# Filler products in TensorE's waits, selections transposed by DMA and new load prices in a planned attention and FFN kernel

## The chip, the cores and the metric

The kernel runs on one core of a Trainium2 chip. The metric is the device time of one execution in microseconds; before the change its median is 272.86 us over 8 runs (271.62 to 273.15).

## The reference

Inputs are q, k and v (batch 4, 8 heads, 768 positions, head size 64) and two weight matrices. Attention selects, for every query, 6 of the 24 key chunks of 32 positions, by an upper bound of the scores, and then attends causally to these chunks alone. Its output, 3,072 tokens of 512 values, goes through an FFN of width 2,048 with a squared ReLU.

```python
k_min, k_max = min and max of k over each chunk of 32
ub = sum_d max(q * k_min, q * k_max)             # bound per query and chunk
ub = where(causal, ub, -1e9)
top_chunks = argsort(ub)[..., -6:]
scores = q @ k.T / 8, where the key's chunk is selected and the key is not later
attn = softmax(scores) @ v
h = maximum(x @ w_in, 0)
out = (h * h) @ w_out
```

## The kernel before

**Tiles.** A sequence is cut into 6 tiles of 128 positions. The first tile of each sequence has fewer than 6 earlier chunks, so it needs no selection: `first_attention` handles it alone for all four sequences, and the FFN of these four tiles (`x_first`) runs first. The remaining five tiles are handled in 16 head pairs (4 sequences of 4 pairs). For each pair `stage_a` prepares and `stage_b` attends.

**Stage A** has this chain: keys and queries transposed (kT, qT), chunk minima and maxima (kr, DVE), positive and negative parts of the queries (qp, qm), the bounds by TensorE (ub), the mask (ubm), the best eight by DVE (m), the comparison that writes the 0/1 selection (selb, L628), its transpose (sT, `turn_selection`, L574 and L632: three TensorE transposes into a PSUM buffer of tag "ps"), and four copies (`copy_selection`, L578) into rows 64 to 87 of the query operand qsc. There a product with −32768 in the key operand kqc switches off the chunks that are not selected. For sequences 0 and 1 keys and queries are transposed by TensorE; for 2 and 3 (`BY_DMA = 2`) by DMA transposes that SP issues (`turn_by_dma`, L328), from staging buffers of tag "nt", of which there are six, or for the first keys from the tile `k0` (`load_turned`, L353).

**Stage B** does, for each head, five score blocks of 512 columns (ps, L679), exponentials by ACT (e, L701), causal masking by DVE or GpSimd, values (av, L690), and the division (x, L521). **The FFN** transposes x (xt, or by DMA for sequences 1 and 2), then `up` (ph, L763; ReLU on ACT or DVE; the square h on DVE) and `down` (py, L793; copy ob; store by SP). For the four first tiles `up` runs in two halves of 256 tokens.

**Order.** Nothing is ordered by hand. Class `Plan` holds every operation with its possible engines and costs, its due time, its inputs and its buffers. `order()` simulates the five engines, the buffer slots of each tag and a single DMA queue, and takes the operation that can start first, among near ties the one due first. The program is written in the order of planned starts, and each engine executes its own part strictly in that order. The planner has these prices: a TensorE operation that starts before `WARM` = 23.5 us costs double (L118); a load takes 0.98 ns a packet (L124), in the order of the string `loads` (i and o are blocks of w_in and w_out, q, k, v are head pairs of sequence 0, F the first tiles of sequences 2 and 3). At most eight GpSimd loads are in flight (L98). `lead` says how long before a pair's stage B its stage A is due; 20 units are one pair. `f_due` is the due time of the first attention of sequences 2 and 3, and `half` is the number of w_in blocks of 128 columns that the first FFN handles in halves. At the very start `warm_up` issues eight products of the all-ones tile `warm`.

The steps below touch L118 to L125 (planner), L145 (`write`), L185 (`P`), L328 to L369 (DMA transposes), L386 to L395 (weight loads), L450 to L458 (warm-up), L545 and L632 (selection).

Of the kernel before, what the change touches and what calls it, by code (L numbers as in the profile page):

```python
# [32 lines left out]
class Op:  # L33
    def __init__(self, where, due, fn, needs, tiles, packets, turns):
        self.where, self.due, self.fn, self.turns = where, due, fn, turns
        self.needs, self.tiles, self.packets = needs, tiles, packets
        self.engine = None
        self.start = self.end = None


class Plan:
# [7 lines left out]
    HAND_OVER = {"PE": 0.22, "ACT": 0.10, "DVE": 0.10, "POOL": 0.12, "SP": 0.1}  # L49
    BUSY = 0.09  # L50
    WAIT = 0.06
    WARM = 23.5
    NEVER = 1e9

    def __init__(self, slots):
        self.slots = slots
        self.ops = []
        self.loads = []

# [10 lines left out]
    def order(self):  # L70
        free = {e: 0.7 for e in ("PE", "ACT", "DVE", "POOL", "SP")}
        slots = {tag: [0.0] * n for tag, n in self.slots.items()}
        waiting = {}
        count = {}
        for op in self.ops:
            for t in op.tiles:
                t.left = len(t.users)
            count[op] = len(op.needs)
            for n in op.needs:
                waiting.setdefault(n, []).append(op)  # L80
        ready = [op for op in self.ops if not count[op]]
        landed, queue, done = [], 0.0, []
        while ready:
            found = []
            for op in ready:
                if op.packets and not op.turns and op is not self.loads[len(landed)]:
                    continue
                at = 0.0
                new = {}
                for t in op.tiles:  # L90
                    if not t.held:
                        new[t.tag] = new.get(t.tag, 0) + 1
                for tag, n in new.items():
                    at = max(at, sorted(slots[tag])[n - 1]
                             if n <= len(slots[tag]) else self.NEVER)
                if at == self.NEVER:
                    continue
                if op.packets and not op.turns and len(landed) >= 8:  # L98
                    at = max(at, landed[-8])
                for engine, cost in op.where.items():  # L100
                    st = max(at, free[engine])
                    for n in op.needs:
                        same = n.engine == engine and not n.packets
                        lag = (0.0 if engine == "PE" else self.BUSY) if same                             else self.HAND_OVER[n.engine]
                        st = max(st, n.end + lag)
                    for t in op.tiles:
                        if t.psum:
                            for e, end in t.last.items():
                                if e != engine and "PE" not in (e, engine):
                                    st = max(st, end + self.HAND_OVER[e])  # L110
                    found.append((st, op, engine, cost))
            assert found, "nothing can start"
            first = min(found, key=lambda f: f[0])
            st, op, engine, cost = min(
                (f for f in found if f[2] == first[2] and f[0] <= first[0] + self.WAIT),
                key=lambda f: (f[1].due, f[0]))
            ready.remove(op)
            if engine == "PE" and st < self.WARM:  # L118
                cost *= 2
            op.engine, op.start, op.end = engine, st, st + cost  # L120
            free[engine] = op.end
            if op.packets:
                queue = max(queue, op.end + (0.7 if op.turns else 1.3))
                queue += op.packets * 0.00098  # L124
                op.end = queue + (0.85 if op.turns else 0.35)  # L125
                if not op.turns:
                    landed.append(op.end)
            for t in op.tiles:
                if not t.held:
                    t.held = True  # L130
                    slots[t.tag].remove(min(slots[t.tag]))
                t.last[engine] = max(t.last.get(engine, 0.0), op.end)
                t.left -= 1
                if not t.left:
                    slots[t.tag].append(
                        max(u.end + self.HAND_OVER[u.engine] for u in t.users))
            for n in waiting.get(op, ()):
                count[n] -= 1
                if not count[n]:
                    ready.append(n)  # L140
            done.append(op)
        assert len(done) == len(self.ops), "operations left"
        return sorted(done, key=lambda op: op.start)

    def write(self):  # L145
        for op in self.order():
            for t in op.tiles:
                if t.tile is None:
                    t.tile = t.make()
            op.fn(op.engine)  # L150


@with_exitstack
def kernel(
# [9 lines left out]
    nc = tc.nc  # L164
# [17 lines left out]
    QC = 128 * NS  # L182
    VW = 80
    NSET = 4
    P = dict(lead=[26, 30, 30, 22, 30, 30, 30, 30, 30, 28, 34, 30, 30, 26, 28, 30],  # L185
             f_due=-123.64, up_due=-21.43, up_rate=3.78, half=10,
             due=[6, 16, 14, 6], rate=[2.42, 2.39, 2.73, 2.66],
             va=5.42, vm=1.3, ra=0.29, h2=1.53,
             loads="i0 q0 k0 F v0 i2 i1 k1 q1 v1 k2 "
                   "v2 o0 q3 i3 q2 k3 o1 v3 o3 o2")  # L190

    nc.scalar.preload_act_table_set("natural_log_exp_and_others")

# [13 lines left out]
    plan = Plan({"tp": 1, "ps": 3, "av": 2, "ff": 2, "e": 6, "h2": NFI + 6, "ht": 3,  # L207
                 "ob": 3, "kq": 6, "nt": 6,
                 "vn": B - 1, "x": 2, "xT": 2,
                 "kr": 2, "qp": 2, "qm": 2, "ubm": 2, "m8": 2, "rc": 2})  # L210
    POOLS = {"tp": pst, "ps": pss, "av": psav, "ff": psf, "e": epool, "h2": hpool,
             "ht": hpool, "ob": opool, "vn": ld, "nt": ldt, "kq": tpool}

# [111 lines left out]
                turned[nm, b] = buffer("kq", [128, NT if nm == "k" else NS, NP, 128],  # L325
                                       name=nm + "t")

    def turn_by_dma(dst, src, due, needs, tiles):  # L328
        return plan.op({"SP": 1.2}, due, lambda _: nc.sync.dma_start_transpose(
            out=dst(), in_=src()), needs, tiles, packets=1070, turns=True)  # L330

    def load_by_sp(nm, due):

# [19 lines left out]
    def load_turned(nm, b, j, due):  # L353
        dst = turned[nm, b]
        if j == 0:
            src, needs = None, loaded[nm, b, "first"]
        else:
            src = buffer("nt", [128, H, D])
            load((nm, b, j), lambda _: nc.gpsimd.dma_start(
                out=src.tile,  # L360
                in_=SRC[nm][b, :, 128 * j:128 * (j + 1)].rearrange("h p d -> p h d")),
                due, 1024, [src])
            needs = loaded[nm, b, j]
        i = j if nm == "k" else j - 1
        op = turn_by_dma(
            lambda: dst[:, i],
            lambda: (src.tile if src else firsts[nm][:, b]).rearrange(
                "p h d -> p (h d)"), due, needs, [src, dst])
        loaded.setdefault((nm, b), []).append(op)  # L369
# [14 lines left out]
    def load_w_in(f0, f1, due):  # L384
        cols = slice(128 * f0, 128 * f1)
        load(("in", f0 // 4), lambda _: nc.gpsimd.dma_start(  # L386
            out=w_in_sb[:, :, cols],
            in_=moe_w_in[:, cols].rearrange("(ki p) f -> p ki f", p=128)),
            due, 2450, cost=0.76)

    def load_w_out(f0, f1, due):
        load(("out", f0 // 4), lambda _: nc.gpsimd.dma_start(
            out=w_out_sb[:, f0:f1],
            in_=moe_w_out[128 * f0:128 * f1].rearrange("(fi p) d -> p fi d", p=128)),
            due, 2450, cost=0.76)  # L395

    def key_tile(nm, b, hp, j):
        t = firsts[nm][:, b] if j == 0 else nat[nm, b][:, j - 1]
# [32 lines left out]
    for b in range(1, B):  # L431
        ones(b, 20 * NP * b - 70)
        for i, nm in enumerate("kq"):
            for j in range(1, NT) if b < BY_DMA else ():
                load_tile(nm, b, j, 20 * NP * b - 70 + 5 * i + j)
            for j in range(0 if nm == "k" else 1, NT) if b >= BY_DMA else ():
                load_turned(nm, b, j, 20 * NP * b - 70 + 5 * i + j)
        for j in range(1, NT):
            load_tile("v", b, j, 20 * NP * b - 60 + j)
# [7 lines left out]
    t_first = {}  # L447
    x_done = {}

    def warm_up(n):  # L450

        wt = psav.tile([128, 4, 128], F32, tag="av", name="wt")
        for _ in range(n):
            nc.tensor.matmul(wt, lhsT=warm,
                             rhs=warm.unsqueeze(1).to_broadcast([128, 4, 128]),
                             start=True, stop=True)

    made["warm"] = plan.op({"PE": 1.7}, -999, lambda _: warm_up(8), [made["vector"]])  # L458

    def first_transposes(nm, b, tag, due):  # L460
        pt = buffer(tag, [128, NP, 128], name="T0")
# [68 lines left out]
    def stage_a(p):  # L530
# [11 lines left out]
        ub = buffer("ps", [128, NS, 2, NC], F32, name="ub")  # L542
        ubm = buffer("ubm", [128, NS, 2, NC], F32)
        m8 = buffer("m8", [128, NS, 2, 8], F32)
        sT = buffer("ps", [128, NT // 2, 128], name="sT")  # L545

        def part(t, rows=slice(0, 128)):
            return t[rows, :, hp] if b >= BY_DMA else t[rows]
# [62 lines left out]
        else:  # L611
# [17 lines left out]
            selbs[:, s, 0:NS, :, 0:NC], ubm.tile,  # L629
            m8[:, :, :, TOPK - 1:TOPK].to_broadcast([128, NS, 2, NC]),  # L630
            op=ALU.is_lt), m + prepared.get((p - NSET, "sT"), []), [ubm, m8])
        t = op({"PE": 0.17}, t0 + 21, turn_selection, [sel, made["ident"]], [sT])  # L632
        prepared[p, "sT"] = [t]
        cs = [[op({"DVE": 0.33, "ACT": 0.385}, t0 + 23 + 2 * hh,
                  lambda e, hh=hh, i=i: copy_selection(e, hh, i),
# [248 lines left out]
```

## Time and profile before

| | |
|---|---|
| median of 8 runs | 272.86 us |
| profiled execution | 272.9 us, of it span 271.2 us |
| mean granted TensorE clock | 0.98 |
| busy PE / DVE / ACT / POOL | 254.6 / 201.8 / 179.6 / 102.7 us |
| chain that ended last | PE 48%, DVE 39%, DMA 8% |
| loads by GpSimd's queue | 13.37 MB in 77,088 packets |

The span runs from the first to the last instruction of one profiled execution. Busy time of PE is matmul time; matmuls are pipelined, so two that overlap are counted once, and a busy PE need not be one at its peak rate. PEld is the loading of the stationary operand, beside it. The granted clock is the share of full speed that the throttle gave TensorE. Rows of groups give line, engine, operation, output and input with shapes, the count, total busy time and the mean of one in ns. Rows of the timeline begin with start and duration in us and end with the idle time before them and what released it.

### The profile page before, as it was taken

The numbers are of one execution on the slowest core, as the hardware profiler recorded it, in microseconds if no ns is written. First come the engines' busy times: TensorE is split into PE (matmuls) and PEld (weight loads), VectorE is DVE, ScalarE is ACT, GpSimd is POOL, SyncE is SP. The second block draws the span as 40 slices with busy tenths as digits, with TensorE's granted clock in tenths as the row PEclk, the third lists the DMA queues.
The fourth block names the chain that finished last, engine by engine and source line by source line (L and its number), as shares of the span: only waits on it lengthen the run. The fifth ranks groups of instructions, "written<-read, shape, count | busy, mean of one in ns | idle before, by whom it ended". The sixth has DMA issues, their size and how long they took to land.

```text
span 271.2 us, 6595 instructions
## 1 busy us (share of the span) xinstructions
PE 254.6 (94%) x2424; PEld 165.0 (61%) x2424; DVE 201.8 (74%) x712; ACT 179.6 (66%) x359; POOL 102.7 (38%) x176
## 2 busy tenths in 40 slices
PE   7478799999999999999899999999999999999994
PEld 2255685666678766555577665567866556665441
DVE  4468699988999999999999999665899524345000
ACT  4356699968888888566578886556888634467111
POOL 8885688898459935812122221001111100000000
PEclk9859999999999999999999999999999999999999
DMA  9999999999999998991520001183000020110111
GB/s 120 180 164 176 137 142 181 195 156 193 172 153 117 152 141 88 164 145 41 116 60 2 2 0 41 41 119 98 2 0 2 1 80 39 41 40 0 41 77 77
DMA packets 100301, 25.07 MB, mean 92 GB/s; under 512 B 92932, under 2 KB 97196, under 8 KB 100268
## 3 DMA queue, kind: packets, MB, share of 16 engines
q0 software_dynamic: 77088, 13.37, 67.6%
q1 hardware_dynamic: 23180, 11.27, 19.9%
q8 instruction: 19, 0.31, 0.5%
q14 instruction: 14, 0.11, 0.1%
HBM read 27.26 MB, written 6.29 MB: 124 GB/s over the span
## 4 chain that ended last, share of the span: by engine, by line
PE 48%; DVE 39%; DMA 8%; POOL 2%; issue 2%; ACT 1%; DVEq 0%; POOLq 0%; ACTq 0%
PE py L793 21%; PE ph L763 16%; DMA w_in_sb<-in_moe_w_in_dram 8%; DVE kr L598 8%; DVE h L781 6%; PE ps L679 5%; DVE qsc L225 4%; DVE kqc L225 4%; PE av L690 3%; DVE m L572 3%; DVE ht L772 3%; DVE x L521 3%; DVE qp L614 2%; DVE qm L614 1%; DVE selb L628 1%
## 5 line engine op out<-in xcount | busy, mean ns | idle before, releaser
L701 ACT ACTIVATE e<-ps 128x512 bf16<-128x512 f32 x160 | 92.8, 598 | 23.9 <-PE ps L679 20.5
L763 PE MATMUL ph<-xT,w_in_sb 128*128 128x256 bf16 (+2 forms) x616 | 101.6, 300 | 2.5 <-DMA w_in_sb<-in_moe_w_in_dram 1.9
L793 PE MATMUL py<-w_out_sb,h 128*128 128x512 bf16 x384 | 95.0, 379 | 0.0
L763 PEld LDWEIGHTS <-w_in_sb 128*128 128x128 bf16 x616 | 57.9, 98 | 25.2 <-DMA w_in_sb<-in_moe_w_in_dram 2.4
L659 POOL TENSOR_SCALAR_AFFINE_SELECT e<-e 128x128 bf16<-128x128 bf16 (+1 forms) x85 | 29.9, 354 | 101.0 <-ACT e L701 99.2
L770 ACT ACTIVATE ht<-ph 128x256 bf16<-128x256 f32 (+2 forms) x113 | 49.7, 443 | 20.3 <-PE ph L763 17.2
L781 DVE TENSOR_TENSOR h<-ht 128x256 bf16<-128x256 bf16 (+2 forms) x154 | 48.1, 326 | 19.5 <-ACT ht L770 12.7
L679 PE MATMUL ps<-qsc,kqc 88*128 88x128 bf16 (+1 forms) x320 | 59.6, 272 | 1.0 <-ACT qsc L223 1.0
L793 PEld LDWEIGHTS <-h 128*128 128x128 bf16 x384 | 35.5, 97 | 30.6
L690 PEld LDWEIGHTS <-e 128*128 128x128 bf16 x640 | 39.1, 97 | 17.7 <-DVE e L656 0.9
L690 PE MATMUL av<-vn,e 128*128 128x65 bf16 x480 | 39.9, 193 | 0.3 <-DVE e L656 0.3
L223 ACT COPY ob<-py 128x512 f32<-128x512 f32 x23 | 13.5, 585 | 24.2 <-PE py L793 24.2
L679 PEld LDWEIGHTS <-kqc 88*128 88x128 bf16 x320 | 24.0, 98 | 6.7 <-issue 1.1
L772 DVE TENSOR_SCALAR ht<-ph 128x256 bf16<-128x256 f32 (+1 forms) x41 | 18.8, 464 | 1.4 <-PE ph L763 1.1
L521 DVE TENSOR_TENSOR x<-av,rc 128x320 bf16<-128x320 f32 (+1 forms) x40 | 18.9, 471 | 0.6
L656 DVE TENSOR_TENSOR e<-e,tri 128x128 bf16<-128x128 bf16 (+1 forms) x43 | 10.0, 235 | 8.5 <-ACT e L701 8.1
L223 ACT COPY qsc<-sT 24x256 bf16<-24x256 bf16 (+1 forms) x31 | 12.8, 414 | 4.5 <-DVE qsc L225 2.9
L572 DVE MAX8 m<-ubm 128x8 f32<-128x24 f32 x160 | 15.6, 166 | 0.1
L690 PE MATMUL av<-v,e 128*128 128x65 bf16 x160 | 15.3, 193 | 0.0
L598 DVE TENSOR_REDUCE kr<-kT 128x24 bf16<-128x768 bf16 x16 | 14.9, 947 | 0.1
L598 DVE TENSOR_REDUCE kr<-kt 128x24 bf16<-128x768 bf16 x16 | 14.7, 939 | 0.1
L372 POOL DMA_DIRECT2D vn<-in_v_dram x15 | 13.2, 903 | 0.1
(83 smaller groups left out, 243.7 us busy)
## 6 DMA issues: line engine op xcount, KB each, us to landing
out_dram<-ob SPq DMA_DIRECT2D x24, 256.0 KB, 2.0
w_in_sb<-in_moe_w_in_dram POOLq DMA_DIRECT2D x4, 512.0 KB, 9.6
w_out_sb<-in_moe_w_out_dram POOLq DMA_DIRECT2D x4, 512.0 KB, 8.0
vn<-in_v_dram POOLq DMA_DIRECT2D x15, 128.0 KB, 6.8
nt<-in_k_dram POOLq DMA_DIRECT2D x10, 128.0 KB, 7.3
nt<-in_q_dram POOLq DMA_DIRECT2D x10, 128.0 KB, 4.9
qn<-in_q_dram POOLq DMA_DIRECT2D x8, 80.0 KB, 8.5
kn<-in_k_dram POOLq DMA_DIRECT2D x8, 80.0 KB, 7.9
```

Source lines behind the costliest of these rows:

```text
L223: nc.scalar.copy(dst, src)
L521: return plan.op({"DVE": 0.06 + 0.00108 * D * n}, due, lambda _: nc.vector.tensor_mul(x(), av[:, :, 0:D], rc[:, 0:n].unsqueeze(2).to_broad ...
L598: nc.vector.tensor_reduce(kr[:, mm].rearrange("d (t c) -> d t c", c=128 // CH) if b >= BY_DMA else kr[:, mm], part(kT).rearrange("d t (c j ...
L659: nc.gpsimd.affine_select(out=e, in_=e, compare_op=ALU.is_ge, fill=0.0, base=0, channel_multiplier=-1, pattern=[[0, n], [1, 128]])
L679: nc.tensor.matmul(ps[:, 128 * c:128 * (c + nt)], lhsT=kqs[:, s, hh, 128 * j:128 * (j + 1)], rhs=qss[:, s, hh, 128 * (t0 - 1):128 * (t0 - ...
L690: nc.tensor.matmul(av[:, t - 1], lhsT=e[:, 128 * c:128 * (c + 1)], rhs=value_tile(b, h, j), start=(i == 0 and c == 0), stop=(i == len(BANK ...
L701: nc.scalar.activation(e.tile, ps.tile, ACT.Exp, scale=scale), [sc], [ps, e])
L763: nc.tensor.matmul(ph.tile, lhsT=w_in_sb[:, ki, 128 * f:128 * (f + 1)], rhs=xT[:, c0 // 128:c1 // 128, ki], start=(ki == 0), stop=(ki == N ...
L770: nc.scalar.activation(ht.tile, ph.tile, ACT.Relu)
L772: nc.vector.tensor_scalar_max(ht.tile, ph.tile, 0.0)
L781: {"DVE": 0.067 + w / 1920}, at[0] + P["h2"], lambda _: nc.vector.tensor_mul(h2[f][:, c0:c1], ht.tile, ht.tile), [op], [ht, h2[f]])))
L793: nc.tensor.matmul(py.tile, lhsT=h2[f][:, 128 * t:128 * (t + 1)], rhs=w_out_sb[:, f, :], start=(f == 0), stop=(f == NFI - 1))
```

## The change

The planner counts double cost for TensorE only before 8 us. For a TensorE operation that starts before 26 us and takes a new PSUM buffer, it notes how many products of 0.216 us fit between the moment when engine and buffer are free and the operation's start, less 0.3 us. Before such an operation is written, `keep_warm` writes that many products of the all-ones tile into its buffer: matmuls for f32 buffers, four times as many transposes for bf16 buffers. The first warm-up has nine products instead of eight. A load takes 0.83 ns a packet; a w_in block counts 4,150 packets, a w_out block 3,070, a DMA transpose 1,270. The order of loads and the due times are different. The first keys of sequences 2 and 3 are transposed by DMA after those of tile 1 have been loaded, not as soon as they are there. The selections of sequences 2 and 3 are transposed by a DMA that SP issues, into a buffer of tag "nt" in SBUF.

```diff
-    WARM = 23.5
+    WARM = 8.0
+    FILL = 26.0
...
-            if engine == "PE" and st < self.WARM:
-                cost *= 2
+            if engine == "PE":
+                op.fill = 0
+                if st < self.FILL and op.tiles:
+                    room = max([free[engine]] + [
+                        sorted(slots[t.tag])[0] for t in op.tiles
+                        if t.psum and not t.held])
+                    op.fill = max(0, int((st - room - 0.3) / 0.216))
+                if st < self.WARM:
+                    cost *= 2
...
-                queue += op.packets * 0.00098
+                queue += op.packets * 0.00083
...
+            if op.fill:
+                self.keep_warm([t for t in op.tiles if t.psum][0].tile, op.fill)
             op.fn(op.engine)
...
-    P = dict(lead=[26, 30, 30, 22, 30, 30, 30, 30, 30, 28, 34, 30, 30, 26, 28, 30],
-             f_due=-123.64, up_due=-21.43, up_rate=3.78, half=10,
-             due=[6, 16, 14, 6], rate=[2.42, 2.39, 2.73, 2.66],
-             va=5.42, vm=1.3, ra=0.29, h2=1.53,
-             loads="i0 q0 k0 F v0 i2 i1 k1 q1 v1 k2 "
-                   "v2 o0 q3 i3 q2 k3 o1 v3 o3 o2")
+    P = dict(lead=[18, 24, 28, 20, 32, 28, 28, 26, 24, 30, 36, 32, 36, 30, 32, 32],
+             f_due=-222.1, up_due=-24.77, up_rate=4.07, half=11, due=[10, 24, 24, 20],
+             rate=[2.42, 2.62, 2.73, 2.11], va=9.67, vm=0.89, ra=-0.27, h2=0.69,
+             loads="i0 q0 k0 F i2 v0 k1 i1 q1 v2 i3 "
+                   "v1 k2 o0 q2 q3 k3 o1 v3 o2 o3")
...
-    def turn_by_dma(dst, src, due, needs, tiles):
+    def turn_by_dma(dst, src, due, needs, tiles, packets=1270):
...
-            src, needs = None, loaded[nm, b, "first"]
+            src, needs = None, loaded[nm, b, "first"] + loaded[nm, b, 1]
...
+    def keep_warm(dst, n):
+        size = 1
+        for dim in dst.shape[1:]:
+            size *= dim
...
+        if dst.dtype == F32:
+            size = min(size, 512) // 128 * 128 or size
+            for _ in range(n * 512 // size):
+                nc.tensor.matmul(
+                    dst[:, 0:size].rearrange("p (a b) -> p a b", b=min(size, 128)),
+                    lhsT=warm, rhs=warm[:, 0:min(size, 128)].unsqueeze(1).to_broadcast(
+                        [128, size // min(size, 128), min(size, 128)]),
+                    start=True, stop=True)
+        else:
+            for _ in range(4 * n):
+                transpose(dst[:, 0:128], warm)
...
-    made["warm"] = plan.op({"PE": 1.7}, -999, lambda _: warm_up(8), [made["vector"]])
+    made["warm"] = plan.op({"PE": 1.9}, -999, lambda _: warm_up(9), [made["vector"]])
...
-        sT = buffer("ps", [128, NT // 2, 128], name="sT")
+        sT = buffer("nt" if b >= BY_DMA else "ps", [128, NT // 2, 128], name="sT")
...
-        t = op({"PE": 0.17}, t0 + 21, turn_selection, [sel, made["ident"]], [sT])
+        if b >= BY_DMA:
+            t = turn_by_dma(lambda: sT.tile, lambda: selbs[:, s].rearrange(
+                "p t h c -> p (t h c)"), t0 + 21, [sel], [sT], 950)
+        else:
+            t = op({"PE": 0.17}, t0 + 21, turn_selection, [sel, made["ident"]], [sT])
```

## The prediction

> **What bounds it now.** I began with the page's 40 slices (6.78 us each), because the change speaks of a first phase.
>
> ```profile
> PE   7478799999999999999899999999999999999994
> PEclk9859999999999999999999999999999999999999
> DMA  9999999999999998991520001183000020110111
> ```
>
> PE is short of 9 tenths only in the first five slices, once in the middle and in the last; the granted clock dips in the second and third. DMA is near full until about slice 18 (122 us), so loads gate the start. Since busy PE need not be PE at its rate, I checked it in columns. From the timeline: 80 py products in 17.28 us are 216 ns each (512 columns), 64 ph in 10.40 us 162 ns (384), 8 ph rows of 256 columns 109 ns, transposes 55 ns, products of 65 or 48 columns about 36 ns. All matmuls of the kernel at these spacings need some 248 us, the warm-up left out. Now the stretches (columns: window, length, then busy us and count of PE, PEld, DVE, ACT, POOL, then clock, DMA share, GB/s):
>
> ```profile
> 0.00:30.00 30.00, 19.54 (x178) 12.22 (x179) 17.97 (x74) 13.38 (x24) 21.14 (x30) 0.83 1.75 157
> 30.00:80.00 50.00, 49.63 (x569) 33.93 (x568) 47.60 (x171) 43.67 (x89) 38.56 (x59) 1.00 1.79 167
> 80.00:155.00 75.00, 72.93 (x750) 49.66 (x748) 74.06 (x253) 57.63 (x119) 34.03 (x62) 1.00 1.08 97
> 155.00:240.00 85.00, 84.96 (x789) 55.37 (x790) 56.43 (x200) 53.65 (x109) 9.02 (x27) 1.00 0.14 37
> 240.00:267.70 27.70, 27.56 (x144) 13.80 (x141) 5.74 (x16) 10.76 (x22) 0.00 (x0) 1.00 0.12 48
> ```
>
> At the same spacings the useful products before 30 us need only 12.2 us. So 236 us of products fill 30 to 267.7 us, 237.7 us: **TensorE streams without a gap from 30 us to the end**, though the chain of waits passes through DVE (39%) as well; DVE is 74.06 of 75 us busy in 80 to 155. A gain is therefore either a product taken off PE, or useful work done before 30 us, of which 17.8 us are lost. The last 3.5 us (final copy, store) are untouched.
>
> The clock in windows of 3.41 us, between whose edges (10.88 and 21.12, three windows apart) it changes:
>
> ```profile
> 7.47:10.88 3.41, 2.10 (x32) 1.34 (x32) 1.73 (x6) 1.71 (x4) 3.41 (x4) 1.00 1.52 189
> 10.88:14.29 3.41, 0.38 (x4) 0.24 (x4) 1.04 (x4) 0.35 (x1) 2.26 (x3) 0.50 2.07 175
> 14.29:17.71 3.42, 2.44 (x23) 2.01 (x23) 2.02 (x5) 1.49 (x3) 3.40 (x5) 0.50 2.36 167
> 17.71:21.12 3.41, 3.29 (x28) 2.59 (x29) 3.05 (x8) 2.30 (x5) 1.71 (x2) 0.50 2.12 171
> 21.12:24.54 3.42, 2.67 (x32) 1.62 (x30) 3.08 (x18) 2.08 (x5) 2.57 (x3) 1.00 1.34 163
> ```
>
> and where PE stood in between:
>
> ```profile
> 10.94 0.38 PE L497 MATMUL av<-v,e 128*128 128x65 bf16 x4 [0.34 <-DVE rc L519]
> 14.92 0.69 PE L228 MATMUL qT<-ident,qn 128*128 128x128 bf16 x5 [3.60 <-DMA qn<-in_q_dram]
> 15.64 0.62 PE L228 MATMUL xt<-ident,x 128*128 128x128 bf16 x4
> 29.03 0.61 PE L763 MATMUL ph<-xT,w_in_sb 128*128 128x256 bf16 x4 [1.85 <-DMA w_in_sb<-in_moe_w_in_dram]
> ```
>
> Three losses are visible. (a) 3.60 us of idleness before 14.92, until query load q0 has landed; queued behind it, in order, stand the last av of sequence 1 and the transposes xt, which needed no load: the old plan expected q0 earlier than it came. (b) At clock 0.50 PE ran 14.92 to 21.12: products worth 3.1 us took twice that. (c) 1.85 us before 29.03, until w_in block i1 has landed.
>
> **Part 1: filling.** Each PE operation that starts before the plan's 26 us and takes a new PSUM buffer is preceded by products of the all-ones tile into that buffer, (wait − 0.3 us)/0.216 of them. PE idles 8.6 us of the first 26 (busy figures of 2-us windows), so about 35 products at most. On an idle PE they cost nothing; if they outlast the wait they push their operation. From above: the eight warm-up products took 3.33 us, 416 ns each, so products that run cold take double, and 7 us would be the worst. From below: nothing. I take 0.3 us, since by my count of load prices (below) data come later than planned, which makes fills too short rather than too long.
>
> Does it hold the clock? [...] The row 7.47:10.88 shows a fall at its end with PE busy 2.10 of 3.41 us and no gap above 0.52 us. [...] where the waiting operation's buffer is bf16 (T, kT, qT, xt, sT) the filler is transposes. Row 14.29:17.71 [...] transposes for most of 2.44 us, no rise; the rise came after 17.71:21.12, which has ph products. [...] I take two thirds: 2.1 us of 0 to 3.1. At cost 1x instead of 2x after 8 us (WARM from 23.5), the plan also places the av and xt ahead of qT.
>
> **Part 2: loads.** The prices fit the trace better than the old ones: first-tile loads landed at 18.08, 19.76 and 21.43, 1.67 us for 2,048 packets, 0.82 ns each against 0.83 planned and 0.98 before; i1 landed 3.0 us after i2, planned 3.44 instead of 2.40. But summed from the start they still put q0 at about 12.1 us, where it came at 14.9, so the plan stays optimistic there. Order: i2 now precedes v0, k1 precedes i1. The two DMA transposes of the last sequences' first keys (SP issued them at 17.80, for 2.62 us, amid these loads; they landed in 9.7) move behind later loads. An estimate: v0 or k1 is 1,280 packets, 1.04 us; the two transposes are worth 0.8 to 2.5 us of DMA time, I take 1.3 (five xT transposes and the stores at 176 to 184 us used 3.05 us of DMA share, but SP issues one in 1.2 to 1.5 us). i2: 26.0 − 1.04 − 0.9 = 24.1. i1: 29.0 + 1.04 − 1.3 = 28.7. k1, whose transposes ran only at 31.4, comes at about 26, so head pair 1's selection work starts 5 us sooner on a DVE idle 27.9 to 29.8. With f_due −222 the first attention of batches 2 and 3 also comes at once; then the second half's ph products for i0 and i2, 7 of 0.43 us, are ready for gap (c). So (c) returns up to 1.85 us; (a) returns what lies between i0's landing (13.3) and 14.9, 1.5 us of ph products.
>
> Sum of (a)+(b)+(c): 0 to 6.4 us, less 0.3. Useful products must also be digested: each ph of 256 columns costs ACT 0.38 and DVE 0.29 us, and pair 0's selection chain keeps DVE busy 15.7 to 25. I take half, **3.2 us**.
>
> **Part 3: selections by DMA.** For batches 2 and 3 (eight head pairs) three transposes each leave PE:
>
> ```profile
> L228 PE MATMUL sT<-ident,selb 128*128 128x128 bf16 x48 | 5.4, 220 | 0.9 <-DVE selb L628 0.8
> ```
>
> 24 of 48, at 55 ns of streaming (not the 220 ns latency): **1.3 us**, all on the bounding engine. Eight DMA transposes come onto SP, 1.2 us of issue each; nothing hides them but the slack ahead of the scores. Now the selection ends at 118.2, 131.3, 141.5, 155.0, 166.6, 179.9, 192.8, 203.7 us, and the pair's first score runs 5.1, 4.3, 5.9, 5.0, 5.6, 6.1, 4.9, 5.0 us later. xT transposes land in 2.5 us when the queues are quiet, kt in 3.4; with four copies of about 0.35 us on two engines (1.3 us in all, as now) that is 3.9 to 4.8 us. It fits seven or eight times, and the leads are set anew (36 for three of the eight). Gone cover: a transpose behind SP's burst of xT transposes (177.5 to 183.3) waits up to 3.5 us more; FFN products stand ready for PE then. Reading selections from SBUF instead of PSUM: DVE's kqc copies are 356 ns (median) from SBUF, 550 from PSUM for as many elements; 32 copies of 0.32 us might save 0 to 4 us of DVE and ACT, none of it on PE: zero. The freed PSUM buffer: zero.
>
> **Sum.** 3.2 + 1.3 = 4.5 us off the profiled execution's 272.9 us (span 271.2 and 1.7 around it, which is also the median, 272.86): **268.4 us**. Everything else in the plan is reordering of a full PE: zero, estimated ±1 us.
>
> **Rivals.** *Loads swallow it* (18%): clock held, but PE then waits longer for i2 and i1; DMA busy near 100% speaks for it, the work made ready by f_due against. Only the 1.3 us and about 0.5 remain: 271.1. *Start fully used* (16%): 6.1 + 1.3, 265.5 us; needs DVE's idle 12 to 15.6 and 28 to 30 us filled, which k1's earlier landing favours. *Selections late* (9%): copies come after PE's need because SP serves transposes in order. For it: 4.3 us of room for pair 9, against 3.9 to 4.8. Against: the ready FFN work. It decides once the exposed waits exceed 4.5 us, 0.56 us a pair; at 0.9 us a pair, 7.2 − 4.5 gives 275.6. *No effect* (4%): the clock falls at 10.88 as before through transposes as filler, and DVE, full from 80 to 155, gives the 1.3 us back: 272.7. The forecast has 53%.
>
> Range: 265.2 (start fully used, a little better) to 271.5 (just past the load case); no effect and most of the slower case are left out, and a little below. Changes under 0.3%, 0.8 us, can't be told from none. Faster: 53 + 18 + 16 = 87%; same 4%; slower 9%.
>
> **What would show it.** Right: clock 1.00 from 10.88 to 21.12; av and xt before qT; PE useful work up about 3 us before 30 us; no PE gap above 1 us before i1; PE busy in 9 tenths through to the end; sT landings within 4 us of the selection, scores not waiting for qsc. Wrong: clock still 0.5 there, PE gaps at 120 to 210 us released by sT copies, or DVE idle waits for transposes.

## The result, and the profile after

The changed kernel takes **269.15 us** (median of 11 runs, 268.44 to 271.81); the kernel before, over 32 runs, 272.39. The ratio is 0.9885, 95% interval [0.986, 0.991]: 3.1 us faster. The prediction was 268.4 us, range 265.2 to 271.5. The profiled execution took 269.94 us with a span of 268.2.

The page's slices for PE and its clock, first:

```profile
PE   7378999999999999999899999999999999999994
PEclk9779999999999999999999999999999999999999
```

The dip of the clock is shorter and still there. The stretches as before (window, length, busy us and count of PE, PEld, DVE, ACT, POOL, then clock, DMA share, GB/s):

```profile
0.00:30.00 30.00, 21.96 (x225) 15.20 (x226) 19.41 (x79) 17.16 (x33) 23.17 (x35) 0.89 1.71 168
30.00:80.00 50.00, 49.14 (x552) 33.42 (x550) 46.19 (x174) 42.31 (x88) 34.85 (x49) 1.00 1.90 151
80.00:155.00 75.00, 72.94 (x770) 49.86 (x768) 73.39 (x253) 61.02 (x127) 34.69 (x65) 1.00 1.27 108
155.00:240.00 85.00, 84.88 (x751) 54.56 (x750) 52.58 (x187) 53.01 (x107) 9.53 (x29) 1.00 0.16 45
240.00:264.70 24.70, 24.62 (x126) 12.01 (x123) 4.66 (x13) 8.30 (x18) 0.00 (x0) 1.00 0.11 43
```

PE, ACT and DVE all work more in the first 30 us (PE 21.96 us instead of 19.54). Useful products counted at their spacing, counted again in both traces, give 11.8 us before 30 us in the old one (the prediction had 12.2) and 14.7 in the new, **2.9 us more**. The kernel needs 1.3 us less of them altogether (the 24 transposes). Yet PE ends at 264.6 instead of 267.6, 2.95 us sooner and not 4.2: about 1.25 us were lost again after 30 us. Of these the busy figures of the stretches show 0.5 us as idleness of PE (2.6 us there before, 3.1 now).

The clock's windows, and where PE stood (timeline: start and duration in us, and at the end the idle time before):

```profile
7.20:10.61 3.41, 1.88 (x32) 1.23 (x29) 1.37 (x5) 2.35 (x5) 3.41 (x5) 1.00 1.54 197
10.61:14.02 3.41, 0.38 (x4) 0.24 (x4) 1.20 (x5) 0.30 (x1) 2.62 (x3) 0.50 2.03 183
14.02:17.43 3.41, 2.64 (x26) 2.55 (x27) 1.56 (x4) 1.57 (x3) 2.94 (x4) 0.50 2.45 156
17.43:20.85 3.42, 2.95 (x33) 2.49 (x32) 3.42 (x10) 2.69 (x6) 2.36 (x4) 1.00 1.77 186
```

```profile
10.84 0.38 PE L523 MATMUL av<-v,e 128*128 128x65 bf16 x4 [0.56 <-DVE rc L545]
14.79 0.69 PE L239 MATMUL qT<-ident,qn 128*128 128x128 bf16 x5 [3.57 <-DMA qn<-in_q_dram]
15.28 0.43 PE L523 MATMUL av<-v,e 128*128 128x65 bf16 x4
...
16.99 0.82 PE L472 MATMUL ph<-warm 128*128 128x256 bf16 x4
17.87 0.60 PE L793 MATMUL ph<-xT,w_in_sb 128*128 128x256 bf16 x4
...
22.19 0.60 PE L472 MATMUL ps<-warm 128*128 128x512 bf16 x2
...
24.16 0.39 PE L239 MATMUL xt<-ident,warm 128*128 128x128 bf16 x4
```

Two things stand against the prediction's picture. The queries' transposes qT still stand ahead of the last av and the xt, and PE still idles 3.57 us for q0. And the filler (the rows that read `warm`) is three small groups, as long as five products of 512 columns in all, none of them in that gap. The planner of the changed kernel expects q0 at 12.1 us, where it lands at 14.8; it sees no wait to fill, and at 12.2 us it sees qT ready ahead of the last av. The clock falls at 10.61 us and rises at 17.43, one window earlier than in the old trace.

### The profile page after: what moved, and what is told of

Same layout as the page of the kernel before. It is cut to its first block, busy times and chain, and to the rows that moved or that the text cites. A ratio compares the mean times of both kernels' runs of the same rounds, so it can differ in the third digit from the quotient of the medians.

```text
span 268.2 us, 6586 instructions
## 1 busy us (share of the span) xinstructions
PE 253.5 (95%) x2415; PEld 165.0 (62%) x2415; DVE 196.2 (73%) x703; ACT 182.4 (68%) x369; POOL 102.2 (38%) x177
## 4 chain that ended last, share of the span: by engine, by line
PE 62%; DVE 16%; DMA 11%; POOL 4%; ACT 3%; issue 2%; SPq 1%; DVEq 0%; POOLq 0%; ACTq 0%
PE ph L793 23%; PE py L823 22%; PE ps L709 8%; PE av L720 4%; DMA kn<-in_k_dram 4%; DVE kr L624 3%; DMA qn<-in_q_dram 3%; DMA w_out_sb<-in_moe_w_out_dram 3%; DVE h L811 3%; DVE qsc L236 2%; DVE x L547 2%; DVE ht L802 1%; DMA xT<-x 1%; PE xt L239 1%; ACT ht L800 1%
## 5 line engine op out<-in xcount | busy, mean ns | idle before, releaser
L731 ACT ACTIVATE e<-ps 128x512 bf16<-128x512 f32 x160 | 91.3, 601 | 20.4 <-PE ps L709 16.4
L793 PEld LDWEIGHTS <-w_in_sb 128*128 128x128 bf16 x620 | 58.5, 97 | 25.2 <-issue 4.4
L709 PE MATMUL ps<-qsc,kqc 88*128 88x128 bf16 (+1 forms) x320 | 58.5, 272 | 0.7 <-ACT qsc L234 0.4
L234 ACT COPY ob<-py 128x512 f32<-128x512 f32 x24 | 14.1, 586 | 29.3 <-PE py L823 28.6
L234 ACT COPY qsc<-sT 24x256 bf16<-24x256 bf16 (+1 forms) x37 | 15.9, 430 | 4.1 <-DMA sT<-selb 1.8
L624 DVE TENSOR_REDUCE kr<-kt 128x24 bf16<-128x768 bf16 x16 | 14.8, 947 | 0.1
L545 DVE RECIPROCAL rc<-av 128x5 f32<-128x5 f32 (+1 forms) x40 | 7.3, 183 | 9.3 <-PE av L523 5.0
```

The source lines that it names most:

```text
L234: nc.scalar.copy(dst, src)
L624: nc.vector.tensor_reduce(kr[:, mm].rearrange("d (t c) -> d t c", c=128 // CH) if b >= BY_DMA else kr[:, mm], part(kT).rearrange("d t (c j ...
L709: nc.tensor.matmul(ps[:, 128 * c:128 * (c + nt)], lhsT=kqs[:, s, hh, 128 * j:128 * (j + 1)], rhs=qss[:, s, hh, 128 * (t0 - 1):128 * (t0 - ...
L731: nc.scalar.activation(e.tile, ps.tile, ACT.Exp, scale=scale), [sc], [ps, e])
L793: nc.tensor.matmul(ph.tile, lhsT=w_in_sb[:, ki, 128 * f:128 * (f + 1)], rhs=xT[:, c0 // 128:c1 // 128, ki], start=(ki == 0), stop=(ki == N ...
```

## The experiments

Each was timed in five rounds beside the kernel before on the same chip; ratios are to that kernel, with their 95% interval. gap_mm, gap_tr, pe_plus and before_sel ran on another chip than the other experiments. Where executions are grouped by mean granted clock below: the old trace has three 3.41 us windows at half clock and a mean of 0.980, the changed kernel's has two and 0.987. So one takes some 0.6% off the mean, and by estimate 0.98 is about three such windows, 0.987 two, 0.993 one, and 0.997 or more none (the clock also falls after the last product, in the old trace at 270.3 us, 2.7 us after it).

**The changed kernel again**, to set the next three against.

> The changed kernel itself, beside the three below on the same chip, so that they can be set against it. Expected ratio to the kernel before 0.9885, within [0.986, 0.991], with the clock at 0.5 from about 10.6 to 17.4 us.

269.72 us (268.38 to 270.56), ratio 0.9889 [0.985, 0.9928]. The result repeats; the clock fell later, at 13.58 us, and was back at 16.99.

**Without the fillers.**

```diff
-    FILL = 26.0
+    FILL = 0.0
```

> The changed kernel with its filler products left out; the plan and the order of all other work stay the same. In the plan these fillers are only five products of 512 columns (two before the first ph at 14.7 planned, two before a preset, one before an xt). Theory A (my prediction, cut to size: the fillers bring the clock back one 3.41 us window earlier, because they close the hole before the first ph): without them the clock rises at about 20.8 us instead of 17.4, products of 17.4 to 20.8 take twice as long, and the kernel is 1.0 to 1.5 us slower than the changed one. Theory B (the load order and the keys' later transposes closed that hole[...]): clock and time as in the changed kernel, within 0.4 us.

269.97 us, ratio 0.9903 [0.9865, 0.9941]. Against the changed kernel that is +0.3 to +0.8 us, inside the intervals. The mean clock was 0.985 to 0.987 in all 7 executions; with the fillers, 14 of 18 had the same and 4 were at 0.991 to 0.993. Four of 18 against none of 7 is too few to say that these five fillers save a window. Theory A's size falls; B's is not excluded.

**First loads priced from the trace.** The last av and the xt come ahead of qT, and fillers are planned for the true waits (twelve products of 512 columns, counted again; the expectation says ten).

```diff
+                if op is self.first_load:
+                    queue += 1.9
...
-            due, 4150, cost=0.76)
+            due, 5100 if f0 == 0 else 4150, cost=0.76)
```

> The changed kernel with the planner's first loads set to the landing times of the trace (queue 1.9 us later after the first load, first w_in block 5,100 packets instead of 4,150), planned anew with the other numbers unchanged. In the plan the last av and both xt now stand ahead of the queries' transposes qT, and ten filler products are written where there were five. Theory A (loss a of the prediction is a fault of order): av and xt run at about 11.3 us instead of 15.3, the first ph starts when w_in block 0 lands (13.3) instead of at 17.9, and the kernel is 0.5 to 2 us faster than the changed one. Theory B (pair 0's selection chain on DVE from q0 onwards sets the pace, not PE): first ph earlier, time the same within 0.5 us. A new plan can also shift later work by about 1 us either way.

269.12 us, ratio 0.9867 [0.9831, 0.9903]. PE's timeline in this kernel:

```profile
11.61 0.39 PE L242 MATMUL xt<-ident,x 128*128 128x128 bf16 x4
...
12.74 0.60 PE L475 MATMUL ph<-warm 128*128 128x256 bf16 x4
13.42 0.60 PE L796 MATMUL ph<-xT,w_in_sb 128*128 128x256 bf16 x4
14.45 0.44 PE L242 MATMUL qT<-ident,qn 128*128 128x128 bf16 x5 [0.43 <-DMA qn<-in_q_dram]
...
24.97 0.60 PE L712 MATMUL ps<-qsc,kqc 88*128 88x256 bf16 x4
```

The order is repaired, the 3.57 us wait has shrunk to 0.43, the first ph starts at 13.42 instead of 17.87, and the clock never fell in the profiled execution (0.992 to 1.0 in all six). Yet pair 0's first score comes at 24.97, against 25.56 and 24.68 in the two traces of the changed kernel, and the time is at best 0.6 us better. DVE runs from qp with hardly a hole to the selection's end at 22.05:

```profile
14.92 0.49 DVE L643 TENSOR_SCALAR qp<-qT 128x640 bf16<-128x640 bf16 x1 [1.55 <-PE qT L242]
...
21.64 0.41 DVE L657 TENSOR_TENSOR selb<-ubm,m 128x240 bf16<-128x240 f32 x1
```

So theory B, pair 0's chain on DVE after q0, holds for most of it.

**The same order without the fillers.**

> The kernel of late_fill, same order, with its ten filler products left out. If fillers hold or bring back the clock once they stand in the right place: the clock's rise is one or two windows of 3.41 us later than in late_fill, and the time 1 to 2 us longer. If the order alone does it: no difference above 0.4 us.

270.12 us, ratio 0.9901 [0.9868, 0.9934]: 1.0 us slower than late_fill in the medians, with overlapping intervals. The clock fell for one or two windows in every execution. Set beside no_fill (269.97), which differs from it by the order alone, it shows what the order is worth without fillers: PE's wait for q0 falls from 3.7 to 0.2 us, and the time stays.

**Filler in the gap, matmuls** (the changed kernel's order).

```diff
...
+        gap = next(op for op in ops if op.fn.__name__ == "turn_queries")
...
+            if op is gap:
+                av = next(t for o in ops[i:] for t in o.tiles
+                          if t.tag == "av" and t.tile is None)
+                av.tile = av.make()
+                self.keep_warm(av.tile, 8)
```

> The changed kernel, same order, with eight filler products of 512 columns more (16 matmuls of 256 columns into the f32 buffer of the fourth av) written ahead of the queries' transposes qT, where TensorE stands idle from about 11.2 to 14.8 us. At half clock they last 3.4 us, at full clock 1.7, so they don't outlast the wait. If matmuls as filler act on the clock: it is back at 1.0 at the window edge near 14, or never falls, and no product after 14.8 us is slow; mean clock 0.993 or more in most executions, against 0.987 in most of the changed kernel. On the time, Theory A (a slow window costs TensorE about 1.5 us, as the executions of the kernel before show, 271.4 to 271.9 us at mean clock 0.984 to 0.987 and 272.8 to 273.8 at 0.980): 1 to 1.5 us faster than the changed kernel. Theory B (pair 0's chain on DVE sets the pace there): under 0.5 us.

268.52 us (268.20 to 269.30), ratio 0.9836 [0.9803, 0.987]: 0.6 to 1.3 us faster than the changed kernel by medians and ratios, with overlapping intervals. Mean clock 0.992 to 1.0.

**Filler in the gap, transposes.** As before, with `self.keep_warm(op.tiles[0].tile, 8)`, into qT's own bf16 buffer.

> As gap_mm, but the filler is 32 transposes of 128 columns (as many columns, 4,096) into the bf16 buffer of qT, which is what the changed kernel's own filler would be there. [...] If they count: as gap_mm.

268.73 us, ratio 0.9841 [0.9799, 0.9884], clock 0.992 to 1.0 in all six executions. Its timeline and windows:

```profile
11.48 1.95 PE L243 MATMUL qT<-ident,warm 128*128 128x128 bf16 x32
14.60 0.44 PE L243 MATMUL qT<-ident,qn 128*128 128x128 bf16 x5 [1.17 <-DMA qn<-in_q_dram]
```

```profile
6.82:10.23 3.41, 2.14 (x30) 1.27 (x28) 1.04 (x3) 1.22 (x3) 3.41 (x5) 1.00 1.59 175
10.23:13.65 3.42, 2.66 (x44) 2.27 (x44) 1.65 (x6) 1.43 (x3) 2.50 (x3) 1.00 1.77 185
13.65:17.06 3.41, 2.14 (x27) 1.66 (x28) 1.83 (x5) 1.95 (x3) 3.41 (x5) 1.00 2.42 158
17.06:20.47 3.41, 2.94 (x38) 2.62 (x38) 3.32 (x9) 2.68 (x7) 2.10 (x3) 1.00 1.98 179
```

32 transposes of ones take 1.95 us at clock 1.00, and the clock stays at 1.00 through the window that holds little else (10.23 to 13.65) and on from there. In the changed kernel, without them, it fell to 0.50 at 10.61. **As filler, transposes held the clock as well as matmuls did** (0.992 to 1.0 in all six executions of either run); whether they alone can raise it, no run here isolates.

**TensorE loaded on purpose.** 96 products of 128 columns of ones more, after the first 110 us; `add` writes them, and 950 packets mark a selection's DMA transpose.

```diff
...
+            if self.extra and op.engine == "PE" and new and new[0].tag == "ps" \
+                    and new[0].tile.dtype == F32:
+                self.add(new[0].tile, self.extra)
+                self.extra = 0
...
+            if op.packets == 950:
+                self.extra += 12
```

> The changed kernel, same order, with 12 products of 128 columns more on TensorE (into the next score buffer, before the scores) for each of the eight selections that go by DMA: 96 products of some 55 ns, 5.3 us of TensorE in all. If TensorE has no slack from there to the end, as the prediction says: 4.5 to 5.5 us slower than the changed kernel, so the 24 transposes taken off are worth 24 x 55 ns = 1.3 us. If DVE or waits bound this stretch: under 2 us slower, and the 24 transposes worth under 0.5 us.

272.57 us over 22 runs, ratio 0.9993 [0.9972, 1.0015]: some 3 us slower than the changed kernel for 5.4 us of products (56 ns apart, 96 of them). The stretch that holds them, in the changed kernel and then in this one:

```profile
110.00:212.00 102.00, 100.13 (x1009) 66.33 (x1008) 87.93 (x311) 75.87 (x153) 22.20 (x62) 1.00 0.37 60
```

```profile
110.00:215.00 105.00, 104.87 (x1106) 71.57 (x1105) 87.95 (x310) 76.96 (x153) 21.04 (x61) 1.00 0.39 57
```

PE had 1.87 us of idleness there and 0.13 are left: nearly 2 us were swallowed by holes. PE is close to its limit and not at it. By this slope 24 transposes are worth some 0.7 us and not 1.3, an estimate that takes removed work to count like added work.

**Only the selections by DMA**, on the kernel before.

```diff
...
-        sT = buffer("ps", [128, NT // 2, 128], name="sT")
+        sT = buffer("nt" if b >= BY_DMA else "ps", [128, NT // 2, 128], name="sT")
...
+        if b >= BY_DMA:
+            t = turn_by_dma(lambda: sT.tile, lambda: selbs[:, s].rearrange(
+                "p t h c -> p (t h c)"), t0 + 21, [sel], [sT], 950)
```

> The kernel before with only the selections of sequences 2 and 3 transposed by DMA, planned anew with its old numbers. By the prediction's third part: 1.3 us faster (271.1 at a before of 272.4), a little less where a selection stands behind SP's burst of xT transposes. Rival (selections late): leads unchanged, scores wait for qsc several times, no faster or up to 3 us slower.

272.34 us over 22 runs beside 272.51, ratio 0.9987 [0.9968, 1.0006]: nothing that can be told from no change. The view of the selection's tile (what the engines that use it sat idle for, us and times; then the landing time):

```profile
  DMA sT<-selb: 6.0, 4
...
DMA to landing us min/median/max: 3.8/3.9/3.9
```

A transpose lands in 3.9 us, not the 2.5 of the estimate, and the copying engines sit idle 6.0 us in all before four of the copies. In the old trace 2.1 to 4.5 us lay between a pair's first two copies and its first score in seven of the eight pairs; here it is 0.3 to 1.0 in six. It fits that later scores give back what PE is spared; no run separates this.

**Only filler in the gap**, on the kernel before (the edit of gap_mm).

> The kernel before, same order and loads, with the filler of gap_mm alone: 16 matmuls of 256 columns of the all-ones tile into the fourth av buffer, ahead of the queries' transposes qT, where TensorE idles until about 14.9 us. It prices a held clock by itself. Theory A (a slow window of 3.41 us costs about 1.5 us): mean clock 0.992 or more instead of 0.980 to 0.987, and 1.5 to 3 us faster than before, ratio 0.989 to 0.9945. Theory B (the clock there matters little, loads and pair 0's chain set the pace): under 0.6 us faster, ratio above 0.998.

272.00 us over 22 runs beside 272.28, ratio 0.9994 [0.997, 1.0017], though the clock was held (0.991 or more in 18 executions). Theory A fails here. PE's timeline shows why:

```profile
27.66 0.61 PE L777 MATMUL ph<-xT,w_in_sb 128*128 128x256 bf16 x4 [1.60 <-DMA w_in_sb<-in_moe_w_in_dram]
```

w_in block i1 is still late. What PE gained before 26 us it waits out at 27.66. The executions of the kernel before agree: 55 at mean clock 0.984 to 0.988 have a median of 272.07 us, 5 at 0.991 or more 272.04, 37 at 0.982 or less 273.75. Two windows at half clock go with no loss at all, the third with 1.7 us. That the third window is the cause of these 1.7 us is not shown: two executions of before_gap with a clock of 0.992 and 0.993 took 274.1 and 274.4 us as well, so something else can cost as much.

**Only the order of loads**, on the kernel before, with the first keys' transposes moved later.

```diff
-             loads="i0 q0 k0 F v0 i2 i1 k1 q1 v1 k2 "
-                   "v2 o0 q3 i3 q2 k3 o1 v3 o3 o2")
+             loads="i0 q0 k0 F i2 v0 k1 i1 q1 v2 i3 "
+                   "v1 k2 o0 q2 q3 k3 o1 v3 o2 o3")
...
-            src, needs = None, loaded[nm, b, "first"]
+            src, needs = None, loaded[nm, b, "first"] + loaded[nm, b, 1]
...
```

> The kernel before with only the order of loads of the changed one (i2 ahead of v0, k1 ahead of i1 and so on) and with the first keys of sequences 2 and 3 transposed by DMA after tile 1 has landed; due times, prices, selections on TensorE as before, no filler. By the prediction's second part: the 1.85 us gap ahead of w_in block i1 closes and head pair 1's selection work starts 4 to 5 us sooner, 1 to 2.5 us faster (ratio 0.991 to 0.996). Rival (the order only pays with the due times set for it, f_due above all): within 0.6 us of before.

269.82 us, ratio 0.9897 [0.9858, 0.9937]: **2.5 us faster (1.7 to 3.9 by the interval), four fifths of the whole change**, with no filler, old due times and all selections on TensorE. How much of it belongs to the order and how much to the later transposes was not separated. PE's waits for loads from 12 to 30 us (engine, line and waiter, releaser: us, times, longest):

```profile
PE qT L228 <- DMA qn<-in_q_dram: 3.7, 1, 3.7
PE kT L228 <- DMA kn<-in_k_dram: 1.0, 1, 1.0
```

The 1.85 us wait for w_in is gone; the wait for q0 stays. When the w_in blocks land can be read where GpSimd, which issues the loads, waits for them (i2, then i1):

```profile
24.26 1.70 POOL L379 DMA_DIRECT2D vn<-in_v_dram  x2 [2.81 <-DMA w_in_sb<-in_moe_w_in_dram]
28.94 1.71 POOL L379 DMA_DIRECT2D kn<-in_k_dram  x2 [0.54 <-DMA w_in_sb<-in_moe_w_in_dram]
```

In the old trace these two waits end at 26.03 and 29.26. So i1 is hardly earlier; what fills the gap ahead of it is work with i2 and k1, which land sooner. Pair 1's selection ends at 38.6 us instead of 41.0.

**Selections back on TensorE**, in the changed kernel, planned anew.

```diff
-        sT = buffer("nt" if b >= BY_DMA else "ps", [128, NT // 2, 128], name="sT")
+        sT = buffer("ps", [128, NT // 2, 128], name="sT")
...
-        if b >= BY_DMA:
+        if False:
             t = turn_by_dma(lambda: sT.tile, lambda: selbs[:, s].rearrange(
```

> The changed kernel with all selections transposed by TensorE again, planned anew with its other numbers; all else as changed. If the DMA transposes are worth what pe_plus says of TensorE's slack (5.4 us of products cost about 3 us, so 1.3 us are worth some 0.7): 0.4 to 1.2 us slower than the changed kernel, ratio 0.990 to 0.993. If they give back in waits what they save, as in before_sel: within 0.4 us, ratio 0.987 to 0.990.

272.01 us over 22 runs, ratio 0.9979 [0.9958, 0.9999]: 2.3 to 2.9 us slower than the changed kernel, more than either theory allowed. PE's longest wait after 30 us:

```profile
PE sT L239 <- DVE selb L654: 2.0, 2, 1.7
```

On TensorE a transpose stands in the engine's order: PE idled up to 1.7 us ahead of one, until DVE had written the selection. But these due times were set for DMA transposes, and before_loads, with older ones, is 2.2 us faster than this kernel with its selections on TensorE too. So part of the 2.3 us belongs to the plan, and how much was not separated.

**The plan set anew for true landing times.** The prices of late_fill, with

```diff
-    P = dict(lead=[18, 24, 28, 20, 32, 28, 28, 26, 24, 30, 36, 32, 36, 30, 32, 32],
-             f_due=-222.1, up_due=-24.77, up_rate=4.07, half=11, due=[10, 24, 24, 20],
-             rate=[2.42, 2.62, 2.73, 2.11], va=9.67, vm=0.89, ra=-0.27, h2=0.69,
-             loads="i0 q0 k0 F i2 v0 k1 i1 q1 v2 i3 "
-                   "v1 k2 o0 q2 q3 k3 o1 v3 o2 o3")
+    P = dict(lead=[10, 26, 26, 26, 54, 46, 26, 38, 24, 32, 28, 32, 38, 40, 28, 86],
+             f_due=-335.07,
+             up_due=-22.68,
+             up_rate=3.79,
+             half=10,
+             due=[10, 22, 16, -10],
+             rate=[2.52, 2.02, 2.28, 3.05],
+             va=6.129,
+             vm=3.302,
+             ra=-0.708,
+             h2=0.943,
+             loads='k0 q0 F i2 v0 k1 i0 q1 i1 v2 i3 q2 o0 k2 k3 v1 q3 o1 o2 v3 o3')
```

> The planner of late_fill (first loads priced from the trace), with due times, leads and the order of loads set anew for it: head pair 0's keys and queries are loaded ahead of the first w_in block, so that pair 0's selection chain on DVE can start some 3 us sooner, and three fillers are left. If that chain bounds the start: first score 2 to 3 us sooner than in late_fill and 1 to 2.5 us faster than the changed kernel (ratio 0.979 to 0.985). If not, or if the plan's later part fits the chip worse: ratio 0.985 to 0.992.

268.21 us (267.14 to 269.03), ratio 0.9828 [0.9793, 0.9863]: with gap_mm the best of all, about 1 us ahead of the changed kernel (0.9885) by the medians, the intervals just touching. The first score comes at 23.67, 1.3 us before late_fill's and not 2 to 3; the first ph at 22.12, 8.7 us later, does no harm that shows in the time. The clock fell here for up to two windows. A filler in its remaining gaps was not tried.

## Why the prediction was right, and where it was not

The total lies 0.75 us above the forecast, but the shares were not those forecast: (a), (b) and part 3 fell short and (c) came out larger, so it is partly luck that the sum was met. Of the signs that the text had set for being right, the clock at 1.00 from 10.88 us on and the av and xt ahead of qT did not come.

- **What bounds it.** "Streams without a gap from 30 us to the end" holds within about 2 us in the loaded stretch: pe_plus shows 54% or so of added work in the time. It was right as to where a gain can come from, and too strict as to its price; its own row 80.00:155.00 had 2.07 us of idleness.
- **(a), the gap at q0: up to 1.5 us.** Failed. The step "the plan also places the av and xt ahead of qT" was wrong, although the text had noted that the plan still expects q0 at 12.1 us. When the order was repaired, at most 0.6 us came of it with fillers (late_fill) and nothing without (late_nofill against no_fill). DVE's chain after q0, which leaves hardly a hole in late_fill, is the likely reason: retuned starts it sooner and is about 1 us ahead, though other due times changed with it.
- **(b), the clock: 2.1 us.** Failed in the way it was priced. The two thirds taken of 3.1 us were the author's estimate. "About 35 products at most" became five, worth 0.3 to 0.8 us that no interval confirms. And the 3.1 us were read from an execution with three half-clock windows (clock 0.98), a minority of the kernel before; most have two, which cost nothing there, as before_gap (ratio 0.9994, its interval spans 1) and the grouped executions (272.07 us against 272.04) show. With the loads in order, three comparisons put a held clock at about 1 us: gap_mm and gap_tr against the changed kernel, late_fill against late_nofill, and the changed kernel's own four executions at 0.991 or more (median 268.8 us) against its other 14 (270.0). In each the spreads overlap, so this is likely and not shown.
- **(c), loads: up to 1.85 us, with pair 1 sooner.** Right in mechanism, and larger than it was priced: before_loads alone gives 2.5 us, with i2 at 24.3 (24.1 forecast), i1 at 28.9 (28.7) and k1 at 26.3 (26). Pair 1's selection came 2.4 us sooner where 5 were expected. One sum is wrong: 3.05 is the sum of the DMA shares of four windows of 2 us, which is 6.1 us of DMA time, so the 1.3 us taken for two transposes were less well founded than they look.
- **Start as a whole: 3.2 us.** 2.9 us more useful work before 30 us, close to the estimate, but not in the shares it was made of: by the same count before_loads has 1.4 us of it, and no_fill, the changed kernel without its fillers, 2.1.
- **Part 3, selections: 1.3 us.** The 1.3 us of products did leave PE; about 1.25 us were lost again after 30 us. By itself the step is worth nothing that could be measured (before_sel). The slack that "fits seven or eight times" was counted with a landing of 2.5 us, where it was 3.9 in that kernel; in the changed kernel it took 2.3, and why the two differ stays open. A price that had been left out is the queue: xT transposes now stand behind a selection's. SP's timeline in the changed kernel, and the ph that waits for an xT (sel_pe, with its selections on TensorE, lists no such wait, but neither does gap_mm, where they go by DMA, so this price is small and not in every kernel):

```profile
125.86 2.00 SPq L340 DMA_TRANSPOSE sT<-selb  x1
127.95 1.22 SPq L340 DMA_TRANSPOSE xT<-x  x1
129.29 0.50 SPq L836 DMA_DIRECT2D out_dram<-ob  x1
129.84 5.54 SPq L340 DMA_TRANSPOSE xT<-x  x4
```

```profile
133.13 0.60 PE L793 MATMUL ph<-xT,w_in_sb 128*128 128x256 bf16 x4 [1.04 <-DMA xT<-x]
```

The rival "loads swallow it" described the kernel before better than the changed one: held clock, no gain. The slower rival did not come: in the changed kernel the copying engines sat idle for the transposes 1.8 us in all, against 6.0 in before_sel. That the new leads are the reason fits, and was not tested.

## What to carry to other kernels

A clock or an engine that looks slow before a late transfer can cost nothing until the transfer is early: on the kernel before, holding the clock gave 0.3 us, no more than could be told from none, and the order of loads with the later transposes 2.5 us. Repair the order of loads first, then the clock. Look at several executions before pricing a clock dip (one program here had from none to three half-clock windows), and check in the plan itself how many fillers get written: a planner that is 2.7 us too optimistic about a load plans none for the wait. A step taken off a busy engine is worth its slope there and not its duration: 5.4 us of products added to PE cost some 3 us here, and 1.3 us taken off it in before_sel gave nothing that could be measured. An added load of known size gives an estimate of the slope.

## What the runs showed of the hardware

In each of the ten traces here in which the clock fell near the start, it fell 6.83 us after it had risen, two windows of 3.41 us: it was up from 4.05 to 10.88 us in the old trace, from 3.78 to 10.61 in the changed kernel's. It did so whether PE's long wait was still to come (10.61 us in the changed kernel, the wait beginning at 11.2) or had begun (13.58 in its second trace, the wait beginning at 11.1). With 1.9 us of filler in the wait before that edge (13.39 us in gap_mm, 13.65 in gap_tr) it stayed at 1.00. The rises of these ten traces lie between 3.78 and 6.75 us, and one program, before_gap, had executions with none, one, two and three half-clock windows.

What decides at the edge stays open: PE's mean work over the 6.83 us does not tell the edges with a fall from those without in these traces. Here are those two windows in late_fill, where the clock held at their end, and in late_nofill, where it fell, and then two later windows of before_gap, at whose end it held:

```profile
5.21:12.04 6.83, 4.60 (x60) 2.75 (x58) 3.49 (x12) 3.28 (x7) 6.83 (x8) 1.00 1.78 180
4.45:11.27 6.82, 4.60 (x50) 2.36 (x48) 2.89 (x10) 3.27 (x6) 6.74 (x9) 1.00 1.77 172
12.63:19.45 6.82, 3.82 (x44) 2.61 (x42) 4.69 (x11) 3.59 (x7) 5.71 (x7) 1.00 2.38 163
```

PE was busy 4.60 us in each of the first two, where the clock held once and fell once, and 3.82 in the third, where it held.
